# Six small edits to the order of a planned kernel: another PSUM bank for one transform, other ring lines for split weights and a scratch tile, a normalisation in steps, a longer look ahead

## The chip, the cores and the metric

The program runs on one core of a Trainium2 chip. The metric is device time in microseconds (us) of one execution. The kernel before took 864.19 us as the median of three runs (862.95, 864.19, 864.58).

## The reference

Input is a sequence of 2048 positions by 640 channels. Four layers run one after the other, each with a residual: a gated long convolution (H3), an MLP, the same convolution again, the same MLP again. The convolution's gate is taken from the normalised residual, but what is convolved (`kv`) depends on the inputs alone, so its result is the same in both layers.

```python
def A(q, k, v, shift_k, ssm_k, ssm_D):
    k_shift = causal depthwise convolution of k with 4 taps
    kv = k_shift * v
    y = irfft(rfft(kv padded) * rfft(ssm_k padded))[:S]   # causal, per channel
    y = y + kv * ssm_D
    return q * y

def B(x, w1, w2):
    return relu(x @ w1) @ w2          # 640 -> 1728 -> 640

x = A_q
x = x + A(layernorm(x), A_k, A_v, A_shift_k, A_ssm_k, A_ssm_D)
x = x + B(layernorm(x), B_w1, B_w2)
x = x + A(layernorm(x), A_k, A_v, A_shift_k, A_ssm_k, A_ssm_D)
x = x + B(layernorm(x), B_w1, B_w2)
```

## The kernel before

**Tiling.** The sequence is cut into eight chunks `c` of 256 rows, each of two halves `s` of 128 rows; the channels into five tiles `t` of 128. The convolution works on units of one or two (chunk, channel tile) pairs: `transform` makes a unit's spectra (`at` of the data, `gt` of the filter), `products` multiplies and sums spectra on VectorE and brings the sum back with an inverse transform on TensorE (tile `pq`, line 602). Chunk 0 has three units, (0,0), (0,2) and (0,4), named by their first pair. The MLP (`main`) takes one half chunk at a time for chunks 0 and 1 and whole chunks after that, and runs over seven slices `j` of the hidden width in the order `JS`: `mm1` makes `h` (lines 995 to 1010), ScalarE and VectorE split relu(h) into two f16 parts `hh` and `hl` (lines 1046, 1047), `mm2` multiplies by w2 (lines 979 to 982).

**Weights.** All 28 weight slices (14 of w1, 14 of w2) are loaded as f32 (`ws`, line 675). TensorE sums their squares (`pw`, line 682, one sum for w1 and one for w2); from each sum follows a power-of-two scale `sc` through a short chain (lines 687 to 693: scratch `dg`, `pn`, `wn`, `wnr`, `wpw`, `wsc`). `wsplit` then makes two f16 parts of each slice: the high part on ScalarE (line 709), the low one on VectorE (line 710). `WLAG` says how many slices of w1 the list of splits runs ahead of w2: with 2 it is w1, w1, w1, w2, w1, w2 and so on (two tiles each).

**Order.** Nothing is issued in the order of the program text. Every operation goes to `Plan` with an engine, a modelled cost and a class: `CRIT` (-1) for chunk 0's convolution and the first half's normalisation, `URGENT` 0, `SOON` 1, `BACK` 1.7 for the second half, `CONV` 2 and so on. `Plan.order` then plays the engines through and writes one fixed order per engine. Three rules matter here:

- A tile belongs to a ring of so many buffers, and to a line (`stream`) in it. A tile gets a buffer only when the tiles ahead of it in its own line have theirs and a buffer is free (`fits`). Ring `w` has 30 buffers; raw and split weights stand in one line, all raw ones first. Ring `tr` has two PSUM banks, shared by the transforms' tiles (`pg`, `pt`, `pr`) and by `pq` in a second line. Ring `h` has two PSUM banks, for the spin-up matmuls, `pw` of w1, and then the MLP's `h`. Ring `u` has two buffers, of which `ones` holds one until the second scale is known. Ring `qs` has one buffer.
- Among those that fit, an engine takes the lowest class, then the earliest.
- A reservation (`rooms`): for each waiting `CRIT` operation whose inputs have all been started, an operation of a higher class is passed over if its cost is more than the time until those inputs are ready plus `SLACK` (0.6).

**Normalisation.** `stats` makes the layer norm of both halves: two squares with a sum (line 766), a square root (767), a reciprocal on VectorE (769), one Newton step in nine small ScalarE instructions (lines 772 to 781), planned as one operation, and the normalised rows `xn` (787). `early(0)` calls it for chunk 0. After the gate (649) and the residual (650), `prep(0, 0, (0,))` makes the first MLP's input: sums (817), mean (840), squares (841), centred rows `xc` (842), square root and reciprocal (843, 844), the f16 parts `xh` (845) and `xl` (846), transposes on TensorE (881) and copies to `xT` (887, 885). The second half takes the same lines in class `BACK`, with its transposes by DMA (874).

Of the kernel before, what the change touches and what calls it, by code (L numbers as in the profile page):

```python
# [13 lines left out]
F16 = mybir.dt.float16  # L14
BF16 = mybir.dt.bfloat16
I32 = mybir.dt.int32
AF = mybir.ActivationFunctionType
# [4 lines left out]
P = 128  # L22
S = 2048
D = 640
# [9 lines left out]
NW = 30  # L34
# [6 lines left out]
CLS = (0, 1, 2.2, 2, 2.5, 3)  # L41
DDP = -6.5
CP = (-7, -6, -4.9)
WLAG = 2
POOLMOD = 5
CRIT, SLACK = -1, 0.6
PEOUT = 0.35
# [47 lines left out]
class Plan:  # L95
# [33 lines left out]
    def order(self):  # L129
        engs = sorted({o.eng for o in self.ops})  # L130
        free = dict.fromkeys(engs, 0.0)
        cand = {e: [] for e in engs}
        soon = {e: [o for o in self.ops if o.eng == e and o.prio[0] == CRIT] for e in engs if e != "SP"}
        for o in self.ops:
            if not o.left:
                cand[o.eng].append(o)
        events, dma, n, out = [0.0], 0.0, 0, []

        def fits(o):
            at = {}  # L140
            for t in o.new:
                k = at.setdefault(t.ring, {})
                if sum(k.values()) >= t.ring.free or t.ring.lines[t.stream][k.get(t.stream, 0)] is not t:
                    return False
                k[t.stream] = k.get(t.stream, 0) + 1
            return True

        finish, later = [], []
        now = 0.0
        while n < len(self.ops):  # L150
            if not events:
                stuck = [(o.eng, o.seq, [t.name for t in o.new]) for e in engs for o in cand[e]]
                raise RuntimeError(f"no order: {stuck[:12]}")
            now = heapq.heappop(events)
            while events and events[0] <= now:
                heapq.heappop(events)
            while finish and finish[0][0] <= now:
                _, _, o = heapq.heappop(finish)
                for t in o.tiles:
                    t.left -= 1  # L160
                    if not t.left and t.ring is not None:
                        t.ring.free += 1
                for d in o.outs:
                    if d.eng == "PE" != o.eng and LATE(d):
                        heapq.heappush(later, (now + LATE(d), d.seq, d))
                        heapq.heappush(events, now + LATE(d))
                        continue
                    if d.eng == "PE" == o.eng:
                        continue
                    d.left -= 1  # L170
                    if not d.left:
                        cand[d.eng].append(d)
            while later and later[0][0] <= now:
                _, _, d = heapq.heappop(later)
                d.left -= 1
                if not d.left:
                    cand["PE"].append(d)
            for e in engs:
                if free[e] > now + 1e-9:
                    continue  # L180
                if e == "SP" and dma > now + LAG:
                    heapq.heappush(events, dma - LAG)
                    continue
                best = None
                rooms = [(max(d.ready for d in o.deps) - now + SLACK, o.prio) for o in soon.get(e, ()) if o.left and all(d.start is not None for d in o.deps)]
                for o in cand[e]:
                    if best is not None and o.prio > best.prio:
                        continue
                    if any(o.cost > room and o.prio > prio for room, prio in rooms):
                        continue  # L190
                    if fits(o):
                        best = o
                if best is None:
                    continue
                cand[e].remove(best)
                for t in best.new:
                    t.ring.free -= 1
                    t.ring.lines[t.stream].pop(0)
                best.start = now
                free[e] = now + best.cost  # L200
                end = free[e] + (PEOUT if e == "PE" else 0.08)
                if best.nbytes:
                    dma = max(dma, now + DLAT) + best.nbytes / DBW
                    end = dma + 1.1
                best.ready = end
                if best.prio[0] == CRIT and e in soon:
                    soon[e].remove(best)
                if e == "PE":
                    for d in best.outs:
                        if d.eng == e:  # L210
                            d.left -= 1
                            if not d.left:
                                cand[e].append(d)
                heapq.heappush(finish, (end, best.seq, best))
                heapq.heappush(events, end)
                heapq.heappush(events, free[e])
                out.append(best)
                n += 1
        return out, now
# [11 lines left out]
def tile_h3_mlp(ctx: ExitStack, tc: tile.TileContext, q, kT, vT, shk, hF, hR, dD, w1, w2, cM, cG, out):  # L231
# [10 lines left out]
    def T(pl, tag, bufs, shape, name, dtype=F32, stream=0):  # L242
        if (pl, tag) not in rings:
            rings[pl, tag] = Ring(pl, tag, bufs)
        return Tile(rings[pl, tag], shape, dtype, name, stream)

    def keep(pl, shape, name, dtype=F32):
        t = Tile(None, shape, dtype, name)
        t.t = pl.tile(list(shape), dtype, tag=name, name=name)
        return t  # L250
# [5 lines left out]
    def act(n, fn, reads, writes, prio, extra=0.0):  # L256
        plan.op("ACT", 0.1 + n * 0.00083 + extra, fn, reads, writes, prio)
# [278 lines left out]
    def products(u, at, gt, after):  # L536
# [43 lines left out]
            dve(768, lambda i=i, pd=pd: DVE.tensor_add(acc[:, i], acc[:, i], pd.t), [acc, pd], [acc], pr_)  # L580
        if not after:
            sv = lambda k: acc.r("p c (s b) -> p c s b", s=3)[:, :, k]
        pq = T(ps, "tr", 2, [P, 512], "pq" + nm, stream=1)
        direct = u[-1][0] == 0
        us = []
        for ri in range(2):
# [78 lines left out]
    def norms():  # L665
# [3 lines left out]
        for k, e in ((0, 9), (1, 13)):  # L669
# [13 lines left out]

                    pe(5 * 0.057, f, [t], [pw2], SOON)
            s2, n2, nr, pw, sc = (keep(const, [P, 1], f"{nm}{k}", d) for nm, d in (("ws2", F32), ("wn2", F32), ("wnr", F32), ("wpw", I32), ("wsc", I32)))
            jk = T(mlp, "hl", 2, [P, P], f"dg{k}", stream=1)
            dve(P, lambda jk=jk, pw2=pw2, s2=s2: DVE.scalar_tensor_tensor(jk.t, pw2[:, 0], 1.0, ident.t, op0=ALU.mult, op1=ALU.mult, accum_out=s2.t), [pw2, ident], [jk, s2], URGENT, 0.2)
            pn = T(ps, "x", 1, [P, 512], f"pn{k}", stream=1)
            pe(0.1, lambda pn=pn, s2=s2: PE.matmul(pn[:, 0:1], ones.t, s2.t, start=True, stop=True), [ones, s2], [pn], URGENT)
# [11 lines left out]
    def wsplit():  # L701
        ks = [(JS[x - y * WLAG], y) for x in range(NFP + WLAG) for y in range(2) if 0 <= x - y * WLAG < NFP]
        for j, k in ks:
            for i in range(2):
                t = WSRC[j, k, i]
                w = T(wp, "w", NW, [P, 2, D], f"w{k}_{j}{i}", F16)
                WT[j, k, i] = w
                s = lambda k=k: sc[k].t.bitcast(F32)
                act(D, lambda t=t, w=w, s=s: ACT.activation(w[:, 0, :], t.t, AF.Copy, scale=s()), [t, sc[k]], [w], SOON, 0.09)  # L709
                dve(D, lambda t=t, w=w, s=s: DVE.scalar_tensor_tensor(w[:, 1, :], t.t, s(), w[:, 0, :], op0=ALU.mult, op1=ALU.subtract), [t, sc[k], w], [w], SOON, 0.13)  # L710
                if (j, k) == (NFP - 1, 0):

                    def f(w=w, i=i):
                        b = w.r("p h (b n) -> p h b n", n=P)
                        ACT.activation(b[:, 0, 1 - i :: 2, 64:P], b[:, 1, 1 - i :: 2, 64:P], AF.Copy)

                    act(192, f, [w], [w], SOON)
# [37 lines left out]
    X = {}  # L755
# [1 line left out]
    def small(tag, name):  # L757
        return T(mlp, tag, 2, [P, 2], name)

    def stats(xs, sums, name, S, pr=0):  # L760
        q_ = slice(S[0], S[-1] + 1)
        negm, ssq, sd, r, v, nmr = (small(k, k + name) for k in ("negm", "ssq", "std", "rstd", "var", "nmr"))
        dve(2, lambda: DVE.tensor_scalar(negm[:, q_], sums[:, q_], -1.0 / D, None, op0=ALU.mult), [sums], [negm], pr)
# [4 lines left out]

        dve(0, lambda: DVE.reciprocal(sd[:, q_], sd[:, q_]), [sd], [sd], pr, 0.15)

        def newton():
            ACT.activation(v[:, q_], ssq[:, q_], AF.Identity, scale=-0.5 / D, bias=heps.t)
            cols = [slice(s, s + 1) for s in S]
            for c in cols:
                ACT.activation(r[:, c], v[:, c], AF.Identity, scale=sd[:, c])  # L775
            for c in cols:
                ACT.activation(v[:, c], r[:, c], AF.Identity, scale=sd[:, c], bias=c15.t)
            for c in cols:
                ACT.activation(r[:, c], v[:, c], AF.Identity, scale=sd[:, c])
            for c in cols:  # L780
                ACT.activation(nmr[:, c], r[:, c], AF.Identity, scale=negm[:, c])

        act(0, newton, [ssq, sd, negm, heps, c15], [v, r, nmr], pr, 0.15 + 0.8 * len(S))
        xns = {}
        for s in S:
            xn = T(mlp, "xn", 2, [P, D], f"xn{name}{s}")
# [394 lines left out]

    def early(a):
        sums = load_x(a)
        first[a] = (X[a], stats(X[a], sums, f"A{a}_0", both, URGENT), [keep(const, [P, 1, 3], f"sp{a}_{s}") for s in range(2)])

    early(0)
    cMs = csplit(cMt, 6)
# [109 lines left out]
```

## Time and profile before

| what | value |
|---|---|
| median of three runs | 864.19 us (862.95 to 864.58) |
| the profiled execution's own time | 864.42 us |
| its span, first to last instruction | 862.6 us |
| TensorE matmuls, busy | 843.1 us (98%) |
| VectorE busy | 744.0 us (86%) |
| ScalarE busy | 483.2 us (56%) |
| mean granted TensorE clock | 0.995 |
| first matmul of the MLP (line 995) | starts at 41.30 us |
| last matmul | ends at 857.4 us |

The profile is of one execution. Times in its views count from the first instruction. A timeline row gives start, duration, engine, line, operation, output and inputs, shape, count, and in brackets how long the engine had been idle before it and what ended that. Matmuls overlap in the array, so a matmul's duration is longer than its slot: the distance between two starts is the slot (0.056 us for 128 columns of f16 at full clock). PEclk is the clock that TensorE was granted, as a share of full speed.

### The profile page before, as it was taken

To read this page: it belongs to the slowest core of one execution; us is meant where nothing else is said; L and a number is where in the kernel's file an instruction comes from. 1 tells how busy PE (TensorE), PEld (TensorE's weight loads), DVE (VectorE), ACT (ScalarE), POOL (GpSimd) and SP (SyncE) were. 2 spreads that over 40 slices of the span, in tenths; PEclk is the share of its full clock that TensorE was granted. 3 is DMA by queue.
4 is the path that set the end of the run, shared out by engine and by line. 5 is a ranking of instruction groups with operands and counts; after the bars stand their busy time and mean duration, and the time that the engine had idled before them with its cause. 6 is when DMAs were issued, how large, how long until landed. Compare 5 with 4: busy or idle time off the path is not lost.

```text
span 862.6 us, 19571 instructions
## 1 busy us (share of the span) xinstructions
PE 843.1 (98%) x7738; PEld 662.2 (77%) x7738; DVE 744.0 (86%) x1367; ACT 483.2 (56%) x1121; POOL 46.4 (5%) x57
## 2 busy tenths in 40 slices
PE   9789999999999999999999999999999999999997
PEld 8777888888877877777777777877777767888886
DVE  7989999999989999999999999999887676645543
ACT  6587688446575574637548374735516266727331
POOL 1000000000000101001001010001000000000000
PEclk9899999999999999999999999999999999999999
DMA  9966968998999979798788888797886462110200
GB/s 322 392 199 238 269 212 278 274 310 269 305 282 268 265 231 266 191 263 220 222 243 250 217 237 168 212 247 226 242 294 234 126 208 62 40 24 1 40 23 32
DMA packets 134989, 181.18 MB, mean 210 GB/s; under 512 B 50673, under 2 KB 87281, under 8 KB 134898
## 3 DMA queue, kind: packets, MB, share of 16 engines
q1 hardware_dynamic: 126578, 169.46, 63.4%
q0 software_dynamic: 8320, 10.49, 8.1%
q8 instruction: 60, 0.98, 0.5%
q14 instruction: 31, 0.25, 0.1%
HBM read 123.61 MB, written 35.65 MB: 185 GB/s over the span
## 4 chain that ended last, share of the span: by engine, by line
PE 66%; DVE 16%; ACT 7%; issue 5%; DMA 5%; SPq 1%; POOL 0%; DVEq 0%; POOLq 0%; ACTq 0%
PE h L1007 10%; PE h L1010 10%; PE h L1008 10%; PE o L934 7%; PE o L979 6%; PE o L980 6%; PE o L982 6%; DVE pacc L580 2%; PE oc L980 2%; PE oc L979 2%; DVE pd L579 1%; PE oc L982 1%; DVE hl L1047 1%; DMA Ax<-A 1%; DVE pacc L576 1%
## 5 line engine op out<-in xcount | busy, mean ns | idle before, releaser
L1007 PE MATMUL h<-xT,w 128*128 128x256 f16 (+1 forms) x1290 | 301.6, 252 | 1.6 <-DVE hh L1061 1.3
L1010 PE MATMUL h<-xT,w 128*128 128x256 f16 (+1 forms) x1290 | 301.4, 251 | 0.8 <-DVE w L710 0.6
L1008 PE MATMUL h<-xT,w 128*128 128x256 f16 (+1 forms) x1290 | 301.4, 251 | 0.0
L1008 PEld LDWEIGHTS <-w 128*128 128x128 f16 x1390 | 136.0, 98 | 13.2 <-issue 2.7
L1007 PEld LDWEIGHTS <-w 128*128 128x128 f16 x1390 | 136.0, 98 | 11.0 <-issue 0.6
L980 PE MATMUL o<-w,hh 128*128 128x512 f16 x364 | 137.9, 379 | 1.4 <-DVE w L710 1.4
L979 PE MATMUL o<-w,hh 128*128 128x512 f16 x364 | 138.1, 379 | 0.3 <-ACT w L709 0.3
L580 DVE TENSOR_TENSOR pacc<-pacc,pd 128x768 f32<-128x768 f32 x140 | 133.5, 954 | 0.8
L1010 PEld LDWEIGHTS <-w 128*128 128x128 f16 x1290 | 126.2, 98 | 10.0 <-DVE w L710 1.1
L982 PE MATMUL o<-w,hl 128*128 128x512 f16 x338 | 128.1, 379 | 0.4 <-DVE hl L1047 0.4
L1046 ACT ACTIVATE hh<-h 128x512 f16<-128x512 f32 (+1 forms) x103 | 50.6, 492 | 102.8 <-PE h L1010 101.4
L980 PEld LDWEIGHTS <-hh 128*128 128x128 f16 x728 | 71.2, 98 | 45.9 <-issue 0.6
L979 PEld LDWEIGHTS <-hh 128*128 128x128 f16 x728 | 71.2, 98 | 45.4 <-issue 1.3
L982 PEld LDWEIGHTS <-hl 128*128 128x128 f16 x676 | 66.1, 98 | 43.1 <-DVE hl L1047 2.0
L579 DVE TENSOR_TENSOR pd<-Ax,Gx 128x768 f32<-128x768 f32 x87 | 81.9, 954 | 2.8 <-DMA Gx<-G 2.7
L980 PE MATMUL oc<-w,hh 128*128 128x128 f16 x364 | 79.7, 219 | 0.0
L979 PE MATMUL oc<-w,hh 128*128 128x128 f16 x364 | 79.7, 219 | 0.0
L982 PE MATMUL oc<-w,hl 128*128 128x128 f16 x338 | 74.0, 219 | 0.0
L1047 DVE SCALAR_TENSOR_TENSOR hl<-h,hh 128x512 f16<-128x512 f32 (+1 forms) x103 | 58.1, 564 | 14.8 <-ACT hh L1046 14.5
L382 ACT ACTIVATE tp<-kt,shs 128x256 f32<-128x256 f32 (+1 forms) x78 | 43.5, 578 | 16.8 <-DVE acc L419 15.7
L579 DVE TENSOR_TENSOR pd<-at,Gx 128x768 f32<-128x768 f32 x44 | 41.3, 955 | 1.2 <-DMA Gx<-G 1.2
L400 POOL DMA_DIRECT2D gs<-hr x20 | 19.6, 980 | 367.6 <-ACT rstdA L775 188.1
(225 smaller groups left out, 1564.6 us busy)
## 6 DMA issues: line engine op xcount, KB each, us to landing
Ax<-A SPq DMA_DIRECT2D x91, 384.0 KB, 4.6
Gx<-G SPq DMA_DIRECT2D x91, 384.0 KB, 4.2
G<-gt SPq DMA_DIRECT2D x32, 384.0 KB, 4.2
A<-at SPq DMA_DIRECT2D x32, 384.0 KB, 3.9
y<-Y SPq DMA_DIRECT2D x30, 320.0 KB, 4.3
ws<-in_w SPq DMA_DIRECT2D x28, 320.0 KB, 6.6
x<-in_q SPq DMA_DIRECT2D x16, 320.0 KB, 4.9
out_dram<-x SPq DMA_DIRECT2D x16, 320.0 KB, 2.6
```

The source lines that it names most:

```text
L382: ACT.activation(o[:, i : i + m], kview(i, m, j), AF.Copy, scale=shs[:, t, j : j + 1])
L579: ew(f"mac{j % POOLMOD}", 768, lambda e, pd=pd, av=av, gv=gv: e.tensor_mul(pd.t, av(), gv()), [ax, gx], [pd], pr_)
L580: dve(768, lambda i=i, pd=pd: DVE.tensor_add(acc[:, i], acc[:, i], pd.t), [acc, pd], [acc], pr_)
L934: PE.matmul(b[:, c : c + w], x, y[:, z : z + w], start=done[i] == 1, stop=done[i] == total[i])
L979: PE.matmul(z, hh[:, c], wh[:, d], start=(j == JS[0] and i == 0 and (h == 0 or s == S[0])), stop=False)
L980: PE.matmul(z, hh[:, c], wl[:, d], start=False, stop=end and tail)
L982: PE.matmul(z, hl[:, c], wh[:, d], start=False, stop=end)
L1007: PE.matmul(p[:, z], wh, xv(t, 0), start=b, stop=False)
L1008: PE.matmul(p[:, z], wh, xv(t, 1), start=False, stop=tail and e)
L1010: PE.matmul(p[:, z], wl, xv(t, 0), start=False, stop=e)
L1046: act(2 * R, lambda p=p, hh=hh: ACT.activation(hh.t, p.t, AF.Relu), [p], [hh], URGENT)
L1047: dve(2 * R, lambda p=p, hh=hh, hl=hl: DVE.scalar_tensor_tensor(hl.t, p.t, 0.0, hh.t, op0=ALU.max, op1=ALU.subtract), [p, hh], [hl], URGENT)
```

## The change

1. `WLAG` goes from 2 to 3: the list of splits is w1 four times, then w2 and w1 in turn.
2. The split weights get a line of their own (`stream=4`) in ring `w`.
3. `pq` of unit (0,2) gets its bank from ring `h` (line 2, after the spin-up tile) and no longer from ring `tr`.
4. The scratch tile `dg` of the two weight sums goes from ring `hl` to ring `qs`.
5. The Newton step of `stats` is written as five planned operations where `fine` is set, which is in `early(0)` alone; elsewhere it stays one operation, whose modelled cost goes from 1.85 to 2.0 for two halves and from 1.05 to 1.15 for one.
6. The reservation counts waiting `CRIT` operations whose inputs haven't been started too. Their time is estimated by `when`, up to three `CRIT` operations deep.

```diff
-WLAG = 2
+WLAG = 3
...
+        def when(o, depth=3):
+            if o.start is not None:
+                return o.ready
+            if not depth or o.prio[0] != CRIT:
+                return 1e9
+            return max([now, *(when(d, depth - 1) for d in o.deps)]) + o.cost + 0.08
...
-                rooms = [(max(d.ready for d in o.deps) - now + SLACK, o.prio) for o in soon.get(e, ()) if o.left and all(d.start is not None for d in o.deps)]
+                rooms = [(max(map(when, o.deps)) - now + SLACK, o.prio) for o in soon.get(e, ()) if o.left]
...
-        pq = T(ps, "tr", 2, [P, 512], "pq" + nm, stream=1)
+        pq = T(ps, *(("h", 2) if u[0] == (0, 2) else ("tr", 2)), [P, 512], "pq" + nm, stream=1 + (u[0] == (0, 2)))
...
-            jk = T(mlp, "hl", 2, [P, P], f"dg{k}", stream=1)
+            jk = T(cv, "qs", 1, [P, P], f"dg{k}", stream=1)
...
-                w = T(wp, "w", NW, [P, 2, D], f"w{k}_{j}{i}", F16)
+                w = T(wp, "w", NW, [P, 2, D], f"w{k}_{j}{i}", F16, stream=4)
...
-    def stats(xs, sums, name, S, pr=0):
+    def stats(xs, sums, name, S, pr=0, fine=False):
...
-        act(0, newton, [ssq, sd, negm, heps, c15], [v, r, nmr], pr, 0.15 + 0.8 * len(S))
+        cols = [slice(s, s + 1) for s in S]
+        A, ident_ = ACT.activation, AF.Identity
+        steps = [
+            (0.2, [ssq, heps], [v], lambda: A(v[:, q_], ssq[:, q_], ident_, scale=-0.5 / D, bias=heps.t)),
+            (0.19 * len(S), [v, sd], [r], lambda: [A(r[:, c], v[:, c], ident_, scale=sd[:, c]) for c in cols]),
+            (0.28 * len(S), [r, sd, c15], [v], lambda: [A(v[:, c], r[:, c], ident_, scale=sd[:, c], bias=c15.t) for c in cols]),
+            (0.19 * len(S), [v, sd], [r], lambda: [A(r[:, c], v[:, c], ident_, scale=sd[:, c]) for c in cols]),
+            (0.19 * len(S), [r, negm], [nmr], lambda: [A(nmr[:, c], r[:, c], ident_, scale=negm[:, c]) for c in cols]),
+        ]
+        if fine:
+            for cost, rd, wr, f in steps:
+                act(0, f, rd, wr, pr, cost - 0.1)
+        else:
+            act(0, lambda: [f() for *_, f in steps], [ssq, sd, negm, heps, c15], [v, r, nmr], pr, sum(x[0] for x in steps))
...
-        first[a] = (X[a], stats(X[a], sums, f"A{a}_0", both, URGENT), [keep(const, [P, 1, 3], f"sp{a}_{s}") for s in range(2)])
+        first[a] = (X[a], stats(X[a], sums, f"A{a}_0", both, URGENT, True), [keep(const, [P, 1, 3], f"sp{a}_{s}") for s in range(2)])
```

More of the change, by code (lines that the diff above doesn't have):

```diff
@@ L769, in stats @@
         dve(0, lambda: DVE.reciprocal(sd[:, q_], sd[:, q_]), [sd], [sd], pr, 0.15)
[L771 to L781, printed above, removed]
-        act(0, newton, [ssq, sd, negm, heps, c15], [v, r, nmr], pr, 0.15 + 0.8 * len(S))
+        cols = [slice(s, s + 1) for s in S]
[12 more added lines that the diff above has]
+            act(0, lambda: [f() for *_, f in steps], [ssq, sd, negm, heps, c15], [v, r, nmr], pr, sum(x[0] for x in steps))
         xns = {}
```

## The prediction

> **What bounds the kernel now.** I read the page's busy times and slices, then a table by stretches of the first 54 us, then the timelines of TensorE, ScalarE and VectorE there, then the waits.
>
> ```profile
> PE 843.1 (98%) x7738; PEld 662.2 (77%) x7738; DVE 744.0 (86%) x1367; ACT 483.2 (56%) x1121; POOL 46.4 (5%) x57
> PE   9789999999999999999999999999999999999997
> ```
>
> TensorE has work from end to end, and no edit adds or removes a matmul. So the time is matmul slots plus what TensorE loses by waiting. By distances between starts, it loses about 8 us in all after 70 us and about 12 us between 20 and 70 us. That head is where the edited tiles live.
>
> ```profile
> 36.00:39.00 3.00, 0.00 (x0) 0.00 (x0) 2.33 (x11) 2.52 (x5) 0.00 (x0) 0.88 1.05 375
> 39.00:42.00 3.00, 2.81 (x27) 2.80 (x28) 2.92 (x5) 2.91 (x6) 0.00 (x0) 0.50 1.08 382
> 42.00:45.00 3.00, 3.00 (x31) 3.00 (x29) 1.08 (x2) 2.33 (x5) 0.00 (x0) 0.50 0.80 321
> 45.00:48.00 3.00, 3.00 (x54) 3.00 (x52) 2.51 (x8) 1.34 (x5) 0.00 (x0) 0.98 0.06 22
> ```
>
> Columns: stretch and length, then busy time of TensorE, its weight loads, VectorE, ScalarE and GpSimd, then granted clock and DMA. TensorE stands idle from 36 to 39, and the granted clock then is 0.50 until about 45. VectorE, full before, does 1.08 of 3 us from 42 to 45.
>
> ```profile
> 25.96 0.71 PE L499 MATMUL pr<-sh,cM 128*128 128x128 f32 x4
> 26.80 1.08 PE L602 MATMUL pq<-u,cM 128*128 128x256 f32 x4
> ...
> 33.84 1.88 PE L682 MATMUL pw<-ws 128*128 128x128 bf16 x30
> 39.19 0.71 PE L881 MATMUL xt<-ident,xh 128*128 128x128 f16 x5 [3.46 <-ACT xh L845]
> ...
> 50.37 0.38 PE L980 MATMUL o<-w,hh 128*128 128x512 f16 x1 [0.61 <-DVE w L710]
> ...
> 52.02 0.22 PE L1008 MATMUL h<-xT,w 128*128 128x128 f16 x1
> 52.87 0.23 PE L1010 MATMUL h<-xT,w 128*128 128x128 f16 x1 [0.63 <-DVE w L710]
> ```
>
> The idle stretch ends with xh of the first half; the next stalls wait for weight splits.
>
> ```profile
> 21.06 0.29 ACT L772 ACTIVATE varA<-ssqA,heps 128x2 f32<-128x2 f32 x1
> ...
> 23.09 0.36 ACT L439 ACTIVATE gt<-pg 128x256 f32<-128x256 f32 x1
> ...
> 34.10 0.28 ACT L632 ACTIVATE qs<-pq 128x128 f32<-128x128 f32 x1 [0.37 <-PE pq L602]
> 36.44 0.83 ACT L841 ACTIVATE xl<-x,negmB 128x640 f16<-128x640 f32 x1 [2.06 <-DVE negmB L840]
> ...
> 37.60 0.81 ACT L709 ACTIVATE w<-ws,wsc 128x640 f16<-128x640 f32 x1
> 38.32 0.81 ACT L845 ACTIVATE xh<-xc,rstdB 128x640 f16<-128x640 f32 x1
> ```
>
> ScalarE has 2.06 us with nothing to do just before the first split, and xh then stands behind that split.
>
> ```profile
> 23.95 0.69 DVE L591 TENSOR_TENSOR u<-pacc 128x512 f32<-128x512 f32 x1
> 28.04 0.69 DVE L591 TENSOR_TENSOR u<-pacc 128x512 f32<-128x512 f32 x1
> ...
> 41.41 1.67 DVE L710 SCALAR_TENSOR_TENSOR w<-ws,wsc,w 128x640 f16<-128x640 f32 x2
> 45.27 0.29 DVE L687 SCALAR_TENSOR_TENSOR dg<-pw,ident 128x128 f32<-128x128 f32 x1 [2.19 <-PE pw L682]
> ```
>
> VectorE waits 2.19 us for the second weight sum with no split to do.
>
> **The longer look ahead.** A newly counted `CRIT` operation has an unstarted `CRIT` input, so its room is at least 0.6 + 0.08 + that input's planned cost, of which the smallest in the code is 0.07: never under 0.75. Only planned costs above 0.75 can be held back: squares and xn on ScalarE, low parts of splits and the constant's low part on VectorE, and the Newton block (1.85), which edit 5 cuts up. Beside inputs as short as that none of them is waiting in these timelines. I take 0; the ends are one low split (0.80 by its start distance) earlier or later.
>
> **The Newton step in five.** The same nine instructions, no queue added. Line 439's copy of the second `pg` of (0,4) is ready when that matmul ends (21.84) and runs at 23.09, after the block. Let in between, it comes up to 1.25 us earlier, and with it the transpose (23.75), sh and pr of (0,4). xn of the first half (24.45) moves back by the copies let in, 0.36 each; its reader, the gate at 25.82, comes 0.5 us after xn is done, so one copy is covered by that and a second would cost about 0.25. at of (0,4) isn't read before 28.99. Alone: 0, ends -0.3 and +0.25.
>
> **pq of (0,2) in ring h.** Its u is done at 24.64 (23.95 + 0.69), the first matmul starts at 26.80, after pr of (0,4) has had the bank. The h banks hold only the spin-up (until 7.5) and `pw` of w1 (until 32.8) before the MLP at 41.30. So the first half of pq can start 2.05 us earlier. What is late next is VectorE: between 24.55 and the second u (28.04) it has yd 0.34, two halves of pacc 0.60 each, gate 0.34 and residual 0.35 in class `CRIT`, 2.23 in sum, so u could start at 26.78; two fillers of lower class slip into the gaps between dependent instructions (0.34 each in these rows), which leaves about 0.6 to 1.2. I take 0.9 on the chain that ends in xc (36.45). The sums that it pushes out (0.60 each) fall into the 2.19 us hole at 43. Ends 0 and 2.05.
>
> **dg in ring qs.** Its one buffer holds qs of (0,2) from 30.02 until the second yd reads it at 33.01, which is class `BACK`. dg ran at 32.46 and may have to wait until 33.35: wsc 34.17 becomes 35.05. qs of (0,4) at 34.10 stands behind the same buffer, so its exposure is one dg, 0.21. Both lie beside ScalarE's hole of 2.06. The freed hl buffer serves nothing before 46.29. I take 0; ends 0 and +0.4.
>
> **The split line and WLAG.** The scale stands at 34.2 and ScalarE is free at 34.38, yet the first split runs at 37.60: in the code, split tiles can't have a buffer before the last raw tile has its own. With their own line two high parts (0.72 each) fit the hole, and xh needs not stand behind one: from rstd's end (37.89) to xh (38.32) 0.43. xl waits at 39.25 for a low part in the same way, 0.2. So the MLP starts 0.9 + 0.4 + 0.2 = 1.5 earlier, TensorE's idle stretch shrinking from 3.46 to about 2. Splits compete with `BACK` work of the second half; that is read only by transposes issued at 50.80, covered while w splits are what TensorE waits for. SP issues no more DMAs than before, in the same queue.
>
> With a lag of 3 the fourth w1 pair is split before the scale of w2 is known: 1.6 us of VectorE work goes into the 2.19 hole. After it every w2 pair stands behind as many splits as before. TensorE's waits for that fourth pair go: 0.79 (52.02 to 52.87, against a slot of 0.056), 0.28 and 0.17 just around it, 1.25 in sum. The two waits for the first w2 pair (0.31 and 0.61 before 49.38 and 50.37) stay, since wsc of w2 sets them. Further on, 0.75, 0.46 and 1.25 at 59, 66 and 68 are waits while VectorE is full; it is a little ahead now: -0.3, ends 0 and -2.4.
>
> Beyond 70 us the planner will write another order, if only since the other normalisations' modelled cost goes up (1.85 to 2.0 for two halves); the remaining waits there may grow or shrink, which I take as 0, ends -1.5 and +1.5.
>
> **Sum.** -1.5 - 1.25 - 0.3 = -3.05. The profiled execution took 864.42 (span 862.6 and 1.8 around it), 0.23 above the median: 861.4.
>
> **Rivals.** *The clock stays up.* The granted clock fell after the idle stretch of 3.46 us and was back at 45.1. Between 39.19 and 45.03 some 65 matmuls of 128 columns ran at 0.107 instead of 0.056: 3.2 us. If the shorter stretch leaves the clock at 1.0, that is saved, less what then waits for wsc of w2; at 2.5 net, 858.9. For it: the stretch shrinks by 1.5. Against: fillers (`pw`) are then fewer in it, so it may shrink less, and the clock fell 2.6 us into it. The Trainium skill ("TensorE: Matmul & The Clock Gate", Part 1) states that a free-running window of about 3.4 us decides and that an idle one throttles. By that rule, taken strictly, a stretch of 2 us can't contain an idle window and 858.9 would be the forecast; the trace bears it out only in part, since the window that ended at the drop had matmuls in its first part.
>
> *The gain is swallowed by the second scale.* The last `pw` stands in TensorE's order after a planned arrival of its load, and that time doesn't move. An MLP that starts earlier puts more of mm1 ahead of it: one more slice, 30 matmuls, takes 1.7 us at full clock and 3.2 at half. wsc of w2 then comes 2.4 later, and with it all w2 splits: 861.4 + 2.4 = 863.8, no change. For it: `pw` and h are interleaved from 41 to 45 already. Against: in that time TensorE has the fourth slice to do.
>
> *Slower: the tails behind a new order.* Each MLP's last slice runs ScalarE, TensorE, ScalarE, VectorE in turn (lines 1050, 1059, 1060, 1061). TensorE waited at four of these for 2.2 us in sum, 1.0 at the longest, and 1.25 at 67.77. Some ten tails lie in the mixed stretch up to 320 us, where VectorE is full. If a new order puts convolution work ahead of the six others at 0.85 each, 5.1 is lost: 866.5. It decides once five or six of them wait. For it: VectorE has nothing spare there; against: nothing in the edits touches that stretch by itself.
>
> *The change does little.* The look ahead, dg and Newton are nil already; if fillers also eat the pq gain, 0.6 + 1.25 + 0.3 is left: 862.3, within the forecast's own range (860.0 to 862.9).
>
> **How the numbers follow.** Forecast 0.44, clock 0.16, swallowed 0.23, tails and other losses of order 0.17. A measurement here can tell about 0.2%, 1.7 us. Faster (under 862.5): 0.16 and all but 0.05 of the forecast, 0.55; within: 0.23 + 0.05 = 0.28; slower 0.17. The range 858.6 to 866.0 takes in the first three and leaves out most of the fourth and a tail of the second.
>
> **What would show it.** pq of (0,2) starting near 24.8 in another bank; the copy at line 439 near 21.9; a first high part before 36; eight w1 splits before the second dg, and VectorE's 2.19 us hole gone; xt near 37.7, h near 39.8; no wait for a split at 52.9. It is wrong if xt doesn't move (VectorE's fillers kept the chain), if the second dg comes much later than 45.3, or if waits after 70 us grow beyond 8.

## The result and the profile after

The changed kernel takes 859.37 us (median of four runs, 859.20 to 860.05) against 864.38 before in the same comparison: a ratio of 0.9944, 95% interval 0.9926 to 0.9961, so it is faster. Timed a second time, it took 859.76 against 864.23 (0.9949, 0.9936 to 0.9961). The forecast was 861.4, its range 858.6 to 866.0. The profiled execution took 859.22, 5.20 under the profiled execution before; the rest is about these two unless said otherwise.

The page after, busy times and then the chain that ended last:

```profile
PE 839.9 (98%) x7738; PEld 661.2 (77%) x7738; DVE 743.4 (87%) x1367; ACT 482.9 (56%) x1121; POOL 46.2 (5%) x57
...
PE 85%; DVE 8%; ACT 4%; issue 1%; DMA 1%; SPq 0%; DVEq 0%; ACTq 0%
```

The chain of the kernel before:

```profile
PE 66%; DVE 16%; ACT 7%; issue 5%; DMA 5%; SPq 1%; POOL 0%; DVEq 0%; POOLq 0%; ACTq 0%
```

No count of the first line has changed. Of the chain, 85% is now TensorE (66% before) and 8% VectorE (16%): the kernel waits less.

To see where, I take for every matmul the distance to the next start, less the slot of its shape at full clock (0.056 us for 128 columns of f16, 0.109 for 256, 0.216 for 512, and so on from the trace). The slots add up to 829.5 us in both kernels; the rest is what TensorE loses, by waiting or at a slow clock. It is 25.62 before and 20.41 after, a difference of 5.21, which is the whole gain. Up to 80 us (the head, in what follows) it fell from 17.29 to 14.96 (2.33), after 80 us from 8.33 to 5.45 (2.88).

Of the later 2.88, 1.87 lies between 80 and 320 us, 0.33 between 320 and 480 and 0.78 between 520 and 720; from 480 to 520 it lost 0.10 more. A good part is the last slice of an MLP waiting for ScalarE. The list of TensorE's waits has for it, before and after (us in total, times, longest us):

```profile
PE hb L1059 <- ACT tb L1050: 2.2, 4, 1.0
```

```profile
PE hb L1067 <- ACT tb L1058: 0.8, 2, 0.5
```

One of the four waits before, 0.46, stands in the head at 66.30; so some 0.9 of the 2.88 is here.

The table by stretches after (columns as in the prediction):

```profile
33.00:36.00 3.00, 1.43 (x25) 1.25 (x22) 3.00 (x17) 2.05 (x4) 0.00 (x0) 1.00 0.68 254
36.00:39.00 3.00, 0.67 (x7) 0.67 (x8) 2.64 (x5) 2.96 (x6) 0.00 (x0) 0.59 0.46 130
39.00:42.00 3.00, 2.74 (x27) 2.58 (x25) 2.46 (x4) 2.68 (x4) 0.00 (x0) 0.50 0.99 270
42.00:45.00 3.00, 3.00 (x45) 3.00 (x43) 2.62 (x8) 1.34 (x3) 0.00 (x0) 0.78 1.06 369
```

VectorE's hole from 42 to 45 is closed (2.62 of 3 us, 1.08 before). TensorE still idles ahead of the first transposes and the granted clock is again 0.50, only earlier.

Timeline of TensorE after:

```profile
24.93 1.03 PE L609 MATMUL pq<-u,cM 128*128 128x256 f32 x4
...
32.26 2.17 PE L689 MATMUL pw<-ws 128*128 128x128 bf16 x35
38.33 0.71 PE L889 MATMUL xt<-ident,xh 128*128 128x128 f16 x5 [3.90 <-ACT xh L853]
...
39.84 0.26 PE L1003 MATMUL h<-xT,w 128*128 128x128 f16 x1 [0.26 <-ACT xT L895]
...
54.40 0.38 PE L988 MATMUL o<-w,hh 128*128 128x512 f16 x1 [0.37 <-DVE w L717]
57.73 0.22 PE L1015 MATMUL hb<-xT,w 128*128 128x128 f16 x1 [0.79 <-DVE hl L1055]
62.08 0.22 PE L1015 MATMUL h<-xT,w 128*128 128x128 f16 x1 [1.87 <-DVE hl L1060]
```

pq of (0,2) starts at 24.93 instead of 26.80, the transposes at 38.33 instead of 39.19, the MLP at 39.84 instead of 41.30. The idle stretch has grown from 3.46 to 3.90, since the weight sums ahead of it end 1.3 earlier and the transposes come only 0.86 earlier. The waits for splits at 50 to 53 are gone; one for a split at 54.40 and later ones for VectorE's low parts of h have come.

Timeline of ScalarE after:

```profile
22.14 0.36 ACT L446 ACTIVATE gt<-pg 128x256 f32<-128x256 f32 x1
...
34.15 1.55 ACT L716 ACTIVATE w<-ws,wsc 128x640 f16<-128x640 f32 x2 [0.88 <-DVE wsc L700]
35.61 0.81 ACT L849 ACTIVATE xl<-x,negmB 128x640 f16<-128x640 f32 x1
...
36.74 0.81 ACT L716 ACTIVATE w<-ws,wsc 128x640 f16<-128x640 f32 x1
37.46 0.81 ACT L853 ACTIVATE xh<-xc,rstdB 128x640 f16<-128x640 f32 x1
```

The copy of `pg` comes at 22.14 (23.09 before) and the first split at 34.15 (37.60). But two splits now stand ahead of the first half's squares (line 849) and another still stands ahead of xh.

Timeline of VectorE after:

```profile
35.16 0.55 DVE L850 TENSOR_SCALAR xc<-x,negmB 128x640 f32<-128x640 f32 x1
...
42.04 1.67 DVE L717 SCALAR_TENSOR_TENSOR w<-ws,wsc,w 128x640 f16<-128x640 f32 x2
...
44.49 0.29 DVE L694 SCALAR_TENSOR_TENSOR dg<-pw,ident 128x128 f32<-128x128 f32 x1 [0.39 <-PE pw L689]
```

xc starts at 35.16 (36.45 before), and the wait before the second dg is 0.39 instead of 2.19.

### The profile page after: what moved, and what is told of

It reads as the page before. It is cut to its first block, busy times and chain, and to the rows that moved or that the text cites. A ratio compares the mean times of both kernels' runs of the same rounds, so it can differ in the third digit from the quotient of the medians.

```text
span 857.4 us, 19580 instructions
## 1 busy us (share of the span) xinstructions
PE 839.9 (98%) x7738; PEld 661.2 (77%) x7738; DVE 743.4 (87%) x1367; ACT 482.9 (56%) x1121; POOL 46.2 (5%) x57
## 4 chain that ended last, share of the span: by engine, by line
PE 85%; DVE 8%; ACT 4%; issue 1%; DMA 1%; SPq 0%; DVEq 0%; ACTq 0%
PE h L1015 12%; PE h L1018 12%; PE h L1016 12%; PE o L987 8%; PE o L988 8%; PE o L990 8%; PE o L942 7%; PE oc L987 2%; PE oc L988 2%; PE oc L990 2%; PE pg L466 1%; ACT w L716 1%; PE pq L609 1%; PE hb L1015 1%; PE hb L1016 1%
```

## The experiments

The theory was that the gain is the head's and comes from the transform and the split weights; rivals were that the later order makes it, that splits are hidden, and that the slow clock matters. For each run I give the median of its runs, and from its profile the loss up to 80 us and after it, and how long the granted clock was 0.50 around 40 us, since that turned out to differ between executions. The profiled execution need not be the median one: it took 864.65 in no_cost, the fastest of ten, 866.94 in no_steps (whose ten lie between 866.23 and 874.80) and 865.75 in no_weights; there the losses fall short of those of a median run by 1 to 3.4 us. In the row of spin50, 2.80 are the slots of the 50 matmuls that it adds.

| kernel | time us | loss to 80 us | loss after | slow clock us |
|---|---|---|---|---|
| before | 863.9 to 864.4 | 17.29 | 8.33 | 6.8 |
| changed | 859.37 | 14.96 | 5.45 | 6.8 |
| changed, timed again | 859.76 | 14.84 | 6.14 | 3.4 |
| without edit 3 (no_pq) | 863.44 | 18.84 | 5.62 | 3.4 |
| without edits 1, 2 (no_weights) | 866.88 | 15.49 | 11.46 | 3.4 |
| without edit 5 (no_steps) | 870.37 | 17.10 | 10.89 | 6.8 |
| old later cost (no_cost) | 867.06 | 14.68 | 11.19 | 3.4 |
| cost in between (late_between) | 860.01 | 14.57 | 6.52 | 3.4 |
| without edits 2, 3 (no_pq_no_line) | 872.93 (one run) | 16.13 | 17.84 | 6.8 |
| before with edit 3 (only_pq) | 860.32 | 15.56 | 6.29 | 3.4 |
| before with edits 1, 2, 4 (weights_dg) | 868.39 | 17.40 | 11.42 | 6.8 |
| before with the later cost (before_late) | 863.02 | 15.26 | 9.23 | 0 |
| changed, TensorE kept busy (spin50) | 858.57 | 11.24 + 2.80 | 5.40 | 0 |

There is no run of edit 6 undone alone: the planner then writes the same order on every engine, so it would be the same program.

**Without the transform's move.**

```diff
-        pq = T(ps, *(("h", 2) if u[0] == (0, 2) else ("tr", 2)), [P, 512], "pq" + nm, stream=1 + (u[0] == (0, 2)))
+        pq = T(ps, "tr", 2, [P, 512], "pq" + nm, stream=1)
```

> The changed kernel with edit 3 undone: the inverse transform of (0,2) goes back to ring tr, all else stays. Theory (the head pays by its chain): the transform starts about 2 us later, near 26.8, the first transposes of xh about 0.9 to 1.3 later (39.2 to 39.6 against 38.33), and the time lost by TensorE up to 80 us goes from 15.0 to 15.9 to 16.5; 860.3 to 860.9 if the stretch after 80 us stays as it is. Rival (the order written for later is what counts): the head's loss changes by under 0.5 and the total by whatever the later stalls do, anywhere from 859 to 864.

863.44 (ratio to before 0.9997, 0.9987 to 1.0006): no gain is left. The transposes come at 39.80 and the head loses 18.84, more than the 16.5 that either theory allowed. What was late is the second weight scale, at 53.17. SyncE's timeline in this kernel shows why:

```profile
32.19 0.40 SPq L375 DMA_DIRECT2D kt<-in_kT  x1
40.24 0.33 SPq L682 DMA_DIRECT2D ws<-in_w  x1
...
43.83 0.34 SPq L682 DMA_DIRECT2D ws<-in_w  x1
```

The last two raw slices are issued at 40.24 and 43.83, where the kernel before has its last at 31.50; the last one lands at 50.11. With a line of their own, splits take buffers of ring `w` that the raw slices need. With no_pq the splits start at 34.18 as in the changed kernel, but in this order four of them run one after the other before the chain's next step. To see if it is the line:

```diff
-                w = T(wp, "w", NW, [P, 2, D], f"w{k}_{j}{i}", F16, stream=4)
+                w = T(wp, "w", NW, [P, 2, D], f"w{k}_{j}{i}", F16)
```

> The changed kernel with edits 2 and 3 undone: the transform back in ring tr and the split weights back in the line of the raw ones. Theory (in the kernel with edit 3 alone undone, splits that start early take buffers of ring w, so that the last raw slice of w2, issued at 43.8 and landed at 50.1, holds the second scale until 53.2): the last raw slice is issued by 32 again, the second scale stands by 49, TensorE's loss up to 80 us is 15.5 to 17.3 instead of 18.8. Rival (the late scale comes from the transform's late start, not from the buffers): second scale at 51 or later, loss up to 80 us 18 or more.

The last raw slice is issued at 30.58, the scale stands at 47.82, and the head loses 16.13. So the line holds the loads. In the changed kernel it also does, for one slice (30.34 to 36.58 between the last two issues), but that slice lands at 39.48 and nothing waits for it. The total of this run is another matter: 17.84 are lost after 80 us.

**Without the weights' edits.**

```diff
-WLAG = 3
+WLAG = 2
...
-                w = T(wp, "w", NW, [P, 2, D], f"w{k}_{j}{i}", F16, stream=4)
+                w = T(wp, "w", NW, [P, 2, D], f"w{k}_{j}{i}", F16)
```

> The changed kernel with edits 1 and 2 undone: split weights back in the line of the raw ones, lag 2. Theory: the first high part comes after the last raw tile again (near 37 instead of 34.15), six w1 splits before the second scale, VectorE's hole before the second dg is back (about 2 us), waits for splits near 52 as before; TensorE's loss up to 80 us 1.5 to 2.2 more than the 15.0 of the changed kernel, so 860.9 to 861.6 with the later stretch unchanged. Rival (the transform and the steps made the gain, splits are hidden): loss up to 80 us within 0.5 of 15.0.

The head loses 15.49. That is just within the rival's bound, 0.5 around 15.0, and far from the theory's. Against 14.57 to 14.84 for the three executions of the changed kernel's head with the same 3.4 us of slow clock (after_again, no_cost, late_between), the weights' edits are worth 0.65 to 0.9 there, not 1.5 to 2.2. The kernel is slower than before all the same (1.0030, 1.0017 to 1.0043), and most of that is one wait. TensorE's timeline there:

```profile
485.92 0.39 PE L1015 MATMUL h<-xT,w 128*128 128x256 f16 x1 [2.53 <-DMA xT<-xh]
487.49 0.37 PE L1016 MATMUL h<-xT,w 128*128 128x256 f16 x1 [1.18 <-DMA xT<-xh]
```

An MLP has no input yet. Its four transposes by DMA were issued at 474.8 to 482.9 (470.2 to 475.7 after), behind a residual update at 463.2 (458.8 after), and the last landed at 487.45 (480.99 after). The stretches around it show what follows, clock in the column before the last two:

```profile
483.00:486.00 3.00, 0.47 (x6) 0.24 (x4) 3.00 (x6) 0.00 (x0) 0.00 (x0) 0.92 1.16 294
486.00:489.00 3.00, 1.82 (x9) 1.09 (x10) 3.00 (x6) 0.63 (x1) 0.00 (x0) 0.50 1.10 347
489.00:492.00 3.00, 3.00 (x16) 2.07 (x15) 2.46 (x5) 0.00 (x0) 0.00 (x0) 0.50 1.05 398
```

TensorE stands still from 483.4, the clock halves, and 6.7 us are lost between 480 and 520, against 0.23 in the changed kernel.

**Only the later order.** In the changed kernel the modelled cost of the later normalisations goes back to the old value:

```diff
-            act(0, lambda: [f() for *_, f in steps], [ssq, sd, negm, heps, c15], [v, r, nmr], pr, sum(x[0] for x in steps))
+            act(0, lambda: [f() for *_, f in steps], [ssq, sd, negm, heps, c15], [v, r, nmr], pr, 0.15 + 0.8 * len(S))
```

> The changed kernel, but the one-piece normalisations after the first keep their old modelled cost (1.85 for two halves, 1.05 for one, where the change has 2.0 and 1.15). Not one instruction of the first 50 us moves and none is added anywhere; only the later order can differ. Theory (the gain of the change is the head's): TensorE's loss up to 80 us stays at 15.0 within 0.3 and the time within 1.5 of 859.4. Rival (the later order is worth as much as the head): loss up to 80 us the same, but the stalls after it, 5.5 in the changed kernel and 8.3 in the one before, grow to 7 or more: 861 and above.

The head is the changed kernel's (14.68), the loss after it doubles to 11.19 even in the fastest of ten executions, and the time is 867.06, above before (1.0036, 1.0021 to 1.0051). The rival holds: an order that differs only from 80 us on costs more than the whole change brings. TensorE's waits in it have the late transposes again (us in total, times, longest us):

```profile
PE h L1015 <- DMA xT<-xh: 2.1, 1, 2.1
```

The same on the kernel before, and then a cost in between on the changed one:

```diff
-        act(0, newton, [ssq, sd, negm, heps, c15], [v, r, nmr], pr, 0.15 + 0.8 * len(S))
+        act(0, newton, [ssq, sd, negm, heps, c15], [v, r, nmr], pr, 0.15 + 0.8 * len(S) + (0 if name == "A0_0" else 0.05 + 0.05 * len(S)))
```

> The kernel before, with nothing but the modelled cost of the one-piece normalisations raised from 1.85 to 2.0 and from 1.05 to 1.15, the first one left as it was; the order is the same up to about 115 us. Theory (the part of the gain after 80 us comes from another order of the mixed and later stretches, which a modelled cost alone can bring about): TensorE's loss up to 80 us is that of before, 17.3 within 0.3, and the loss after it, 8.3 in the kernel before and 5.5 in the changed one, comes out elsewhere by a microsecond or more. Rival (the later loss follows from how far the head is ahead): with the head of before the loss after 80 us stays within 1 of 8.3 and the time within 1 of 864.

The loss after 80 us is 9.23 instead of 8.33, within 1, as the rival has it; the waits that make it up are others (the longest, 1.60 at 267.5 us, has no counterpart before), so the run does not decide between the two. The loss up to 80 us was not that of before but 15.26, though the order there is the same; that is the clock, below. Of 1.4 us by the medians (0.9982, 0.9972 to 0.9992) it can't be said how much is order and how much clock.

```diff
-            act(0, lambda: [f() for *_, f in steps], [ssq, sd, negm, heps, c15], [v, r, nmr], pr, sum(x[0] for x in steps))
+            act(0, lambda: [f() for *_, f in steps], [ssq, sd, negm, heps, c15], [v, r, nmr], pr, 0.25 + 0.8 * len(S))
```

> The changed kernel with the modelled cost of the one-piece normalisations after the first between the old and the new (1.95 for two halves, 1.05 plus 0.05 for one... 1.95 and 1.15): the same order up to about 80 us, another after it. Theory (after 80 us it is chance which order comes out, and whether one MLP near 486 us waits for its transposes): loss up to 80 us 14.5 to 15.2, the loss after it anywhere from 5 to 12, with 3 or more of it near 486 us if the residual update of that chunk comes later than about 462 us. Rival (the raised cost as such makes the later order better, and more of it is better still): the loss after 80 us lies between the 11.2 of the old cost and the 5.5 of the new one.

The loss after 80 us is 6.52, between the two as the rival has it, and within what chance allows as well. It is a weaker test than meant, since its order leaves that of the changed kernel only at 187 us and not at 80. But the raised cost by itself does not make a better later order: before_late has it and loses more after 80 us than before, no_weights has it and loses 11.46. In late_between the residual update ahead of the MLP at 486 us comes at 462.0, and no transpose is late.

**Without the steps.** Edit 5 undone, the longer look ahead kept:

```diff
-            act(0, lambda: [f() for *_, f in steps], [ssq, sd, negm, heps, c15], [v, r, nmr], pr, sum(x[0] for x in steps))
+            act(0, lambda: [f() for *_, f in steps], [ssq, sd, negm, heps, c15], [v, r, nmr], pr, 0.15 + 0.8 * len(S))
...
-        first[a] = (X[a], stats(X[a], sums, f"A{a}_0", both, URGENT, True), [keep(const, [P, 1, 3], f"sp{a}_{s}") for s in range(2)])
+        first[a] = (X[a], stats(X[a], sums, f"A{a}_0", both, URGENT), [keep(const, [P, 1, 3], f"sp{a}_{s}") for s in range(2)])
```

> The changed kernel with edit 5 undone: the first Newton step is one operation of 1.85 again, and the other normalisations have their old cost. Theory of the forecast (the steps are worth nothing by themselves): transposes of xh within 0.4 of 38.3 and TensorE's loss up to 80 us within 0.5 of 15.0. Rival (the longer look ahead needs the steps: it holds back an operation of 1.85 for as long as a shorter CRIT operation is near): xn and with it the gate come later, the first weight scale too, the first MLP matmul starts at 41.5 or later against 39.84, and the loss up to 80 us is 16.5 or more.

The rival holds. The first MLP matmul starts at 42.28, the first weight scale stands at 38.24 (33.97 in the changed kernel), and the head loses 17.10 against 14.96 with the same slow clock. In whole, 870.37. The cause is to be seen where the Newton step starts, here and then in the changed kernel:

```profile
28.57 0.29 ACT L781 ACTIVATE varA<-ssqA,heps 128x2 f32<-128x2 f32 x1
```

```profile
19.04 0.30 ACT L781 ACTIVATE varA<-ssqA,heps 128x2 f32<-128x2 f32 x1
```

It started at 21.06 in the kernel before. So the step in one piece stands 7.5 us later than before, though ScalarE has nothing to do for 5.7 us in sum between 20.7 and 28.3. With edit 6 undone as well, the planner puts it back where it was. With an operation of 1.85 in the plan the look ahead is not nil; with the five steps it is.

**The transform alone, and the weights alone,** each on the kernel before:

```diff
-        pq = T(ps, "tr", 2, [P, 512], "pq" + nm, stream=1)
+        pq = T(ps, *(("h", 2) if u[0] == (0, 2) else ("tr", 2)), [P, 512], "pq" + nm, stream=1 + (u[0] == (0, 2)))
```

> The kernel before with edit 3 alone: the inverse transform of (0,2) in ring h. Theory: it starts near 24.9 instead of 26.80 and the transposes of xh come 1.0 to 1.4 before the 39.19 of before; but the first splits stand in the line of the raw weights as before, so the first MLP matmul starts at 41 to 41.5 all the same and the loss up to 80 us is 16.8 to 17.3. Rival (the transform is the main part of the head's gain): first MLP matmul 0.9 or more before 41.30, loss up to 80 us 16.3 or less.

860.32 (0.9947, 0.9932 to 0.9963): one line gives nearly the whole gain. The transposes come at 38.41, but the MLP starts at 40.92, between the two expectations, since the first split still runs at 38.27. The head loses 15.56, as the rival has it (16.3 or less); the loss after it is 6.29 against 8.33. The head's 15.56 has 3.4 us of slow clock in it and the 17.29 of before 6.8, so how much of their difference is the line's stays open; the gain in the medians, 4.1, does not rest on it.

```diff
-WLAG = 2
+WLAG = 3
...
-            jk = T(mlp, "hl", 2, [P, P], f"dg{k}", stream=1)
+            jk = T(cv, "qs", 1, [P, P], f"dg{k}", stream=1)
...
-                w = T(wp, "w", NW, [P, 2, D], f"w{k}_{j}{i}", F16)
+                w = T(wp, "w", NW, [P, 2, D], f"w{k}_{j}{i}", F16, stream=4)
```

> The kernel before with edits 1, 2 and 4: the line of the splits, the lag of 3 and the scratch tile that they need out of ring hl. Theory: first high part before 36.4, eight w1 splits before the second scale; first MLP matmul 0.3 to 0.8 before 41.30 and the waits for the fourth w1 pair (1.2) gone: loss up to 80 us 15.8 to 16.6. Rival (splits early in ScalarE's and VectorE's order stand in the way of the first half's chain, which is not ahead here): transposes of xh no earlier than 39.0, second scale later than the 48.3 of before, loss up to 80 us 17 or more.

The rival holds: transposes at 39.15, the MLP at 41.26, the second scale at 49.92, and a head of 17.40 where before has 17.29. By themselves the weights' edits bring nothing. Edit 4 can't be left out of them: with the line of the splits and `dg` in ring `hl`, the planner comes to a point where nothing can start, so it is there for that and not for time.

**The clock.** 50 matmuls that nobody reads, in the stretch where TensorE waits; every other order is kept:

```diff
+            if not s:
+                warm2 = T(ps, "h", 2, [P, 512], "warm2", stream=5)
+                for _ in range(50):
+                    pe(0.057, lambda: PE.matmul(warm2[:, 0:P], ident16.t, ident16.t, start=True, stop=True), [ident16, sums2], [warm2], IDLE)
```

> The changed kernel with 50 matmuls of 128 columns on the identity added (into a spare bank of ring h, read by nobody), which TensorE runs in the stretch where it waits for xh; the rest of every engine's order is the same. Theory of the clock: the stretch of 3.9 us before 38.3 was what took the granted clock to 0.50 for 6.8 us; with the added matmuls it stays at 1.0, some 50 matmuls behind 38.3 take 0.056 instead of 0.107, and TensorE reaches the wait for the second scale about 2.5 us earlier; of that 0.5 to 2.5 is left at the end: 857 to 859. Rival (the slow clock is hidden behind the splits): the clock stays up, but VectorE sets the pace from 38 to 70 us, so the waits for splits grow by as much and the time stays within 0.5 of 859.4.

858.57 (0.9938, 0.9921 to 0.9954), and then beside the changed kernel on one chip:

> The changed kernel itself, beside the next one on the same chip. Both theories: 859.2 to 860.1, as before.

> The changed kernel with the 50 added matmuls in the stretch before the first transposes, timed on the same chip as the changed kernel. Theory (of the about 2.5 us of matmul slots that the slow clock takes, about 1 is not hidden behind splits): 0.5 to 1.3 under the changed kernel. Rival (hidden, or the added matmuls cost as much as the clock): within 0.4 of it.

859.11 (858.57 to 859.65) against 859.76 (859.33 to 860.52); the two ranges overlap a little. Stretches of the second spin50, and below them of the changed kernel timed beside it:

```profile
33.00:36.00 3.00, 3.00 (x57) 3.00 (x55) 2.99 (x18) 1.73 (x4) 0.00 (x0) 1.00 0.78 291
36.00:39.00 3.00, 1.60 (x29) 1.43 (x27) 2.64 (x6) 2.97 (x7) 0.00 (x0) 1.00 0.36 105
39.00:42.00 3.00, 2.25 (x38) 2.01 (x35) 2.87 (x5) 2.81 (x5) 0.00 (x0) 1.00 0.93 270
```

```profile
36.00:39.00 3.00, 0.09 (x2) 0.10 (x3) 2.64 (x5) 2.97 (x7) 0.00 (x0) 0.98 0.23 56
39.00:42.00 3.00, 2.74 (x26) 2.58 (x27) 2.67 (x4) 2.71 (x4) 0.00 (x0) 0.50 0.99 317
```

The clock stays at 1.00. The head's loss with the added slots is 14.04 and 14.14, against 14.96 and 14.84 with 6.8 and 3.4 us at half: 0.7 to 0.9, and 0.65 at the end by the medians. That is the theory's lower end: TensorE does the same work sooner and then waits more (2.25 of 3 us busy from 39 to 42). spin50 is the fastest of all, by little.

## Why the prediction was right, and where not

The direction and the range held; the way to the number did not, in half of it. The head gave 2.33 where the sum had 3.05, and the later stretch 2.88 where it had 0. That the later part helped was luck: with the same head and another later order, no_cost came out at 867.06, above the whole range.

- **Look ahead: right, but conditional.** Nil beside the five steps, as worked out. But it is not nil beside the step of 1.85, so "Alone: 0" for the Newton step misses what the steps are there for: with the look ahead in, undoing them costs 2.1 in the head. The steps without the look ahead were not run.
- **pq of (0,2): right in mechanism, too small.** The start was forecast near 24.8 and was 24.93; xc moved by 1.29 where 0.9 was taken. That a single edit would carry the total was not seen: alone it gives 860.32.
- **dg in ring qs: right for time.** The first dg ran at 31.44, earlier than before, since qs was free sooner.
- **The split line: half wrong.** "xh needs not stand behind one, 0.43" failed: another split stands there (36.74), again 0.43 after rstd's end, and two more stand ahead of the squares, 0.57 after negm's end (35.04 to 35.61). So the transposes moved by 0.86 and not 1.5. The start of the MLP came out as forecast (1.46 against 1.5) because it no longer waits for the low parts: from transposes to h it takes 1.51 instead of 2.11. "SP issues no more DMAs than before, in the same queue" overlooked that raw slices wait for the buffers that splits take.
- **The lag of 3: right.** Eight high parts run before the second dg, the hole is 0.39, and the 1.25 of waits at 52 is gone. The waits for the first w2 pair are gone too, since wsc of w2 came at 46.67 and not 48.19. But "-0.3" for 55 to 70 us failed: by starts, 0.96 and 2.03 are lost there, 2.99 against 2.95 before.
- **The clock.** "TensorE's idle stretch shrinking from 3.46 to about 2" failed, it grew to 3.90, so that rival's condition did not come about. Its price was 2.5 net; measured, 0.7 to 0.9. The gross price was too high already: 55 matmuls, not some 65, start between 39.19 and 45.03 before, which makes 2.8 us and not 3.2.
- **Beyond 70 us: the term that was mis-sized.** I took 0, ends -1.5 and +1.5; it was -2.88, and over all these kernels the loss after 80 us goes from 5.4 to 17.8. The slower rival looked for waits at tails up to 320 us. Tails are what shrank there in the changed kernel; in the kernels that came out slower the largest waits are near 486 to 490 and 735 us, an MLP without its transposed input, which no rival named.
- **Two readings of the kernel before.** The loss between 20 and 70 us was over 14 us by the measure used here, not about 12. And 861.4 is 3.05 below the profiled execution; from the median of 864.19 the same sum gives 861.1.

So the gain is not the head's alone. What part of 2.88 belongs to which edit stays open: each edit rewrites the order from there on, and a modelled cost that moves nothing in the head changes the later loss by twice as much. Whether the late transposes follow from the late residual update alone is not settled either: it stood at 463 or later in all five kernels that lost 2.5 us or more near 486 to 490 or at 735, but also in two that lost 0.2 there, no_pq and before_late. In these two the last transpose landed at 487.03 and 486.16, and TensorE came to that MLP at 487.24 and 486.44. So it matters too when TensorE comes. That margin, 0.2 and 0.3 us there, is 6.0 in the kernel before (481.70 to 487.65) and 2.2 in the changed one (480.99 to 483.14): the change is faster and stands closer to this wait.

## What to carry to other kernels

Where one list scheduler writes the order of everything, no edit is local: cost the head by its chain, but give the rest of the schedule an error bar taken from two or three orders that differ by a modelled cost alone. Look for the inputs with the least margin (here transposes by DMA, which in the changed kernel land 2.2 us before they are needed) and treat their margin as the risk. A tile with a line of its own starts earlier and takes its buffer from somebody; find out from whom.

## What the runs showed of the hardware

The granted clock changes on a grid. In these traces the time at 0.50 near 40 us is 0, 3.41 or 6.83 us, and the full stretches before it are nine or ten times 3.413. Cutting each trace into such windows, the clock fell after windows in which TensorE was busy for 0.39 of the time or less (0.39 in the changed kernel, 0.24 before, 0.00 to 0.37 in others) and did not after 0.42 in weights_dg (at 485 us) or 0.44 and 0.47 in before_late; it came back after windows of 0.86 or more, and not after 0.74. The Trainium skill ("TensorE: Matmul & The Clock Gate", Part 1) has the free-running window of about 3.4 us, and the traces agree; its idle window need not be idle here, 0.39 busy was enough to lose the clock. Since the grid stands anywhere against the kernel's start, the same order can pay or not. The kernel before, with 3.46 us of idle time, shows 0.50 in the prediction's table; before_late, with the same order up to 115 us, shows this:

```profile
36.00:39.00 3.00, 0.00 (x0) 0.00 (x0) 2.33 (x11) 2.34 (x5) 0.00 (x0) 1.00 1.06 371
39.00:42.00 3.00, 2.37 (x38) 2.19 (x39) 3.00 (x5) 3.00 (x6) 0.00 (x0) 1.00 1.08 389
```

TensorE idles just as long and the clock stays at 1.00; the head then loses 15.26 and not 17.29. So two profiles of one order can differ by 2.0 us in the head with the clock. The 2.33 measured for the head is what the change brings with 6.8 us of slow clock in both kernels; with none in either (before_late and spin50) the heads differ by 1.1 to 1.2. Over whole executions less of it is seen. Of the 60 executions of the kernel before that were timed beside the experiments, the 19 with a mean granted clock of 0.994 or 0.995 took 864.7 us on average, the 28 with 0.997 or 0.998 took 863.9. That sorting is rough, since the clock also stands at 0.50 for 1.9 to 5.0 us behind the last matmul, but 0.8 of a spread from 862.4 to 866.9 is all that goes with the clock there.
